# Starting the second pass of a fused decode-block forward and backward one iteration earlier

## The chip, the cores and the metric

The kernel runs on one core of one Trainium2 chip, as one launch. The metric is device time in microseconds (us), the median of several executions. Two sizes set most of it: tiles of 1 MiB of bfloat16 that are moved between HBM and the on-chip memory, and vector instructions of about 1 us each that work on them.

## What is computed

A transformer block for one decode token per batch row, and its whole gradient. Cut to what matters:

```python
B, D, H, Sk, Dh, Dff = 2, 640, 32, 4096, 128, 1728
def fwd(x, K, V, wq, wo, w1, w2):
    q = layernorm(x) @ wq                        # (B, H, Dh)
    p = softmax(einsum("bhd,bhkd->bhk", q, K) * Dh ** -0.5)
    o = einsum("bhk,bhkd->bhd", p, V)
    h = x + o.reshape(B, H * Dh) @ wo
    return h + relu(layernorm(h) @ w1) @ w2
out, vjp = jax.vjp(fwd, x, K, V, wq, wo, w1, w2)
return out, *vjp(grad_out)    # gradients of x, K, V, wq, wo, w1, w2
```

The caches K and V have 64 (batch, head) pairs of 1 MiB each; their gradients have the same size. Each pair's gradient is an outer product spread over the sequence, so it is written whole.

## The kernel before

**Two passes over the 64 pairs.** The first pass (`p1_iter`, lines 468 to 608) takes one new pair per iteration `i`, software-pipelined over three iterations: pair `i` is transposed on PE and scored, pair `i-1` gets its softmax weights (`ep`, line 540) and its weighted keys `pk` (line 486, on DVE), and pair `i-2` is reduced on PE against V (`m_part`, line 476). Each iteration loads one K and one V tile. The second pass (`p2_iter`, lines 892 to 970) takes head `j`: it needs V once more (tile `W`), and stores the gradients `gV` and `gK`, 1 MiB each, built on DVE at line 868 from the row `rb` (ACT, line 911). The last six V tiles of each batch row stay on chip (`KEPT`), and the second pass takes these first, so its heads run 26 to 31, then 0 to 25.

**The middle.** Between the passes of a batch row `b` stands `middle_gen(b)` (lines 771 to 842): the attention output, a layer norm, the hidden layer, the ReLU mask, the gradient through `w1`, the backward layer norm `ln_bwd` (lines 285 to 315), and then, by groups of heads (`go_group`, lines 711 to 742), the gradient of each head's output. Head `j` of the second pass can't start before its group is done. For batch row 0 the middle begins after iteration 33.

**The order of the work is written out by the program, at build time.** Each engine runs its instructions in the order in which they are emitted. `p1_iter` yields eight times in an iteration (steps k = 0 to 7); after each step the main loop emits some of the second pass, pumps the load queue, and lets the background (`bg`, the middle among it) emit as much as a credit allows: 0.8 a step in iterations 34 to `P2_AT - 1`, 0.2 a step in first-pass iterations from `P2_AT` on. A generator pays 0.5 for a plain yield. `wait(n)` (lines 152 to 157) holds the background back for n steps; it emits nothing. The long vector products of the middle (`ttr`, line 697) also need a slot from `turn()`: between the middle's start and `P2_AT` an iteration gives five (two at k = 1, one each at k = 3, 4 and 6). `bg_until` at the start of a head emits at once whatever that head still needs.

**The steps that matter here.** After the mask (`ghfc`, line 811) and a pause, `spread_some` (lines 655 to 664) turns a piece of `ghfc` into a row: PE transposes (line 661) into a PSUM bank, one copy on ACT (line 663) into `fbc`. Five `ttr` follow on it; this is done three times, with widths 640, 640 and 448. Then `ln_bwd`: sums on DVE, a pause, a column sum on PE (`colsum`, line 226), the rest on DVE; then the row `hbc`, spread in the same way; then `go_group` for heads 26 and 27: two `ttr`, a pause, `pair_rows` (lines 351 and 356), a pause, `d_ps` (lines 727 and 731) and five small DVE instructions to `GQc` (line 739). `csum`, `pr_ps` and `d_ps` all lie in PSUM bank 7 (role "mid").

**The second pass's start.** `P2_AT = H + 2 + M0_ITERS` (line 1182) is the first-pass iteration with head j = 0. From there every second iteration carries a head ("mixed") and the others none ("plain"), until i = 64, from where every step of the plan carries one. So heads stand in iterations 41, 43, ... 63, 64, 65, and heads 14 to 64 follow without a first pass. `P2_AT` also moves the end of the help that ACT gives with `pk` (`PK_ACT`, line 480), the engine of two small copies (lines 501 and 580), a K tile that goes over to the second pass (line 582), a PSUM bank (line 1284), the doubling of pauses (line 1312) and the start of batch row 1's output sums (line 1308).

**Transfers.** Loads are issued on SP's queue in one list (`queue`, lines 1197 to 1226), as soon as one of 13 homes of 1 MiB is free; during the mixed stage the stores are issued on POOL's queue. While six kept V tiles are held, seven homes are left for K and V. A K home comes free after the second `pk` instruction (line 582), a V home after line 604.

Of the kernel before, what the change touches and what calls it, by code (L numbers as in the profile page):

```python
# [15 lines left out]
def kernel(  # L16
# [41 lines left out]
    def f_kc(c):  # L58
        return 128 if c < NFF else F_rem
# [92 lines left out]
    def wait(n):  # L152

        end = step[0] + n * spread[0]
        while step[0] < end and not forced[0]:
            yield 0.0
        yield
# [34 lines left out]
    x2c = cols.tile([128, ND, B], BF16)  # L192
    rstd2 = cols.tile([128, B], FP32)
    gc = cols.tile([128, ND, B], BF16)
    h1c = cols.tile([128, ND, B], BF16)
    gh1c = cols.tile([128, ND, B], BF16)
# [26 lines left out]
    def colsum(src, n):  # L223

        t = pst([128, 16], FP32, "mid", "csum")
        nc.tensor.matmul(t[:, 0:n], lhsT=ones_f32, rhs=src, start=True, stop=True)
        return t

    def bc(ap, n):
        return ap[:, :, None].to_broadcast([128, ap.shape[1], n])  # L230
# [51 lines left out]
        nc.vector.tensor_tensor(out=xh.rearrange("p c b -> p b c"), in0=y_bf[:], in1=bc(rstd, ND), op=ALU.mult)  # L282
        yield from wait(3)

    def ln_bwd(gh, xh, rstd, add, dst, nb):

        lb = small if nb == 1 else fin
        def t3(name):
            return lb.tile([128, nb, ND], FP32, tag=f"lb_{name}{nb}", bufs=1, name=f"lb_{name}")
        xh_v = xh.rearrange("p c b -> p b c")  # L290
        prod = t3("prod")
        nc.vector.tensor_tensor(out=prod[:], in0=gh, in1=xh_v, op=ALU.mult)
        mm = lb.tile([128, 2, nb], FP32, tag=f"lb_mm{nb}", bufs=1, name="lb_mm")
        nc.vector.reduce_sum(out=mm[:, 0, :], in_=gh, axis=AX.X)
        nc.vector.reduce_sum(out=mm[:, 1, :], in_=prod[:], axis=AX.X)
        yield from wait(2)
        t = colsum(mm[:].rearrange("p a b -> p (a b)"), 2 * nb)
        yield
        nm = lb.tile([128, 2, nb], FP32, tag=f"lb_nm{nb}", bufs=1, name="lb_nm")
        nc.vector.tensor_scalar(out=nm[:].rearrange("p a b -> p (a b)"), in0=t[:, 0:2 * nb],  # L300
                                scalar1=-1.0 / D, scalar2=None, op0=ALU.mult)
        u1 = t3("u1")
        if nb == 1:
            nc.vector.scalar_tensor_tensor(out=u1[:, 0, :], in0=xh_v[:, 0, :], scalar=nm[:, 1, 0:1], in1=gh[:, 0, :],
                                           op0=ALU.mult, op1=ALU.add)
            nc.vector.tensor_scalar(out=u1[:, 0, :], in0=u1[:, 0, :], scalar1=nm[:, 0, 0:1], scalar2=rstd,
                                    op0=ALU.add, op1=ALU.mult)
        else:
            nc.vector.tensor_tensor(out=u1[:], in0=xh_v, in1=bc(nm[:, 1, :], ND), op=ALU.mult)
            nc.vector.tensor_tensor(out=u1[:], in0=u1[:], in1=gh, op=ALU.add)  # L310
            nc.vector.tensor_tensor(out=u1[:], in0=u1[:], in1=bc(nm[:, 0, :], ND), op=ALU.add)
            nc.vector.tensor_tensor(out=u1[:], in0=u1[:], in1=bc(rstd, ND), op=ALU.mult)
        nc.vector.tensor_tensor(out=dst.rearrange("p c b -> p b c"), in0=u1[:],
                                in1=add.rearrange("p c b -> p b c"), op=ALU.add)
        yield from wait(3)
# [298 lines left out]
    def o_group():  # L614
        b, g = divmod(o_next[0], H // OG)
        hs = slice(g * OG, g * OG + OG)
        nc.vector.tensor_tensor(out=OU[:, b, hs], in0=OU[:, b, hs], in1=rt[:, b, hs], op=ALU.mult)
        nc.vector.tensor_copy(out=OFc[:, hs, b], in_=OU[:, b, hs])
        o_next[0] += 1

    def a_group():

        b, g = divmod(a_next[0], H // OG)
        a_ps = pst([128, ND], FP32, "mid", "a_ps")
        for c in range(ND):
            for h in range(g * OG, g * OG + OG):
                nc.tensor.matmul(a_ps[:, c:c + 1], lhsT=wo_t[:, h, c * 128:(c + 1) * 128], rhs=OFc[:, h, b:b + 1],
                                 start=(h == g * OG), stop=(h == g * OG + OG - 1))
        nc.vector.tensor_tensor(out=asum[:, b, :], in0=asum[:, b, :], in1=a_ps[:], op=ALU.add)
        a_next[0] += 1  # L630
# [17 lines left out]
    def wide_row(name):  # L648
        return cols.tile([128, B * D], BF16, tag="wide_row", name=name)
# [121 lines left out]
    def middle_gen(b):  # L771
        if o_next[0] < (b + 1) * H // OG:
            o_group()
        u4[0] = wide_row("u")[:, 0:256].bitcast(FP32)
        nc.vector.tensor_reduce(out=u4[0], in_=u_bank[0][:].rearrange("p (s d) -> p d s", s=4),
                                axis=AX.X, op=ALU.add)
        yield
        if b:
            yield from wait(2)
        while a_next[0] < (b + 1) * H // OG:  # L780
            if a_next[0] == o_next[0]:
                o_group()
                yield
                yield
            a_group()
            yield
        at_bf = small.tile([128, ND], BF16, tag="at_bf", bufs=1, name="at_bf")
        nc.vector.tensor_copy(out=at_bf[:], in_=asum[:, b, :])
        nc.vector.tensor_tensor(out=h1c[:, :, b], in0=xg32[:, b, :], in1=at_bf[:], op=ALU.add)
        h32 = small.tile([128, 1, ND], FP32, tag="h32", bufs=1, name="h32")  # L790
        nc.vector.tensor_copy(out=h32[:, 0, :], in_=h1c[:, :, b])
        yield ("a", b)
        u_out(b)
        yield from ln_fwd(h32[:], 1, x2c[:, :, b:b + 1], rstd2[:, b:b + 1])
        wide = 32
        hf_w = pst([128, NF, wide], FP32, "mid", "hf_ps")
        hf_ps = hf_w[:, :, 0]
        for cf in range(NF):
            kc = f_kc(cf)
            for c in range(ND):  # L800
                nc.tensor.matmul(hf_w[0:kc, cf, :], lhsT=w1_t[:, c, cf * 128:cf * 128 + kc],
                                 rhs=x2c[:, c, b:b + 1].to_broadcast([128, wide]),
                                 start=(c == 0), stop=(c == ND - 1))
            yield 0.25
        nc.vector.tensor_scalar(out=acol[:, 0:NFF, b], in0=hf_ps[:, 0:NFF], scalar1=0.0, scalar2=None, op0=ALU.max)
        if F_rem:
            nc.vector.tensor_scalar(out=acol[0:F_rem, NFF, b:b + 1], in0=hf_ps[0:F_rem, NFF:NF],
                                    scalar1=0.0, scalar2=None, op0=ALU.max)
        mask = small.tile([128, NF], FP32, tag="mask", bufs=1, name="mask")
        nc.vector.tensor_single_scalar(out=mask[:], in_=acol[:, :, b], scalar=0.0, op=ALU.is_gt)  # L810
        nc.vector.tensor_tensor(out=ghfc[:, :, b], in0=ga[:, b, :], in1=mask[:], op=ALU.mult)
        yield from wait(3)
        fbc = wide_row("fbc")
        gx2 = small.tile([128, 1, ND], FP32, tag="gx2", bufs=1, name="gx2")
        gx2p = small.tile([128, ND, 3], FP32, tag="gx2p", bufs=1, name="gx2p")
        first_f = 0
        for k, n in enumerate((ND, ND, NF - 2 * ND)):
            row = fbc[:, (k % 2) * D:(k % 2 + 1) * D]
            w = spread_some(one(ghfc, b), k * ND, n, f_kc, row)
            yield  # L820
            for c in range(ND):
                yield from turn()
                part = w1_t[:, c, first_f:first_f + w]
                ttr(part, row[:, 0:w], gx2p[:, c, k:k + 1], w, part if b else later_heads())
                yield 0.85
            first_f += w
        nc.vector.reduce_sum(out=gx2[:, 0, :], in_=gx2p[:], axis=AX.X)
        yield ("w1", b)
        yield from ln_bwd(gx2[:], x2c[:, :, b:b + 1], rstd2[:, b:b + 1], gc[:, :, b:b + 1], gh1c[:, :, b:b + 1], 1)
        row = wide_row("hbc")  # L830
        hbc, junk = row[:, 0:D], row[:, D:2 * D]
        spread_some(one(gh1c, b), 0, ND, lambda c: 128, hbc)
        yield
        yield ("gh1", b)

        first = H - KEPT[b]
        bounds = [(first, first + 2), (first + 2, H)] if b == 0 else [(first, H)]
        bounds += [(h, min(first, h + GH)) for h in range(0, first, GH)]
        for h0, h1 in bounds:
            yield from go_group(b, h0, h1, hbc, junk)  # L840
        if b > 0:
            yield from mlp_out()
# [335 lines left out]
        forced[0] = False  # L1178

    EARLY = 2  # L1180
    M0_ITERS = 7
    P2_AT = H + 2 + M0_ITERS
    RATES = (0.2, 0.8, 0.2, 0.8, 0.45)
    RATE2 = 0.65
# [180 lines left out]
```

## Time and profile before

| what | value |
|---|---|
| median of 3 runs | 884.89 us (884.12 to 885.16) |
| the profiled execution | 885.37 us, span 883.6 us |
| busy share of the span: PE, DVE, ACT, POOL | 83%, 77%, 56%, 19% |
| moved by DMA | 361.86 MB, mean 410 GB/s |
| iterations 34 to 40 (middle of batch row 0) | some 44 us, about 207 to 251 us of the span |
| iteration 41 (mixed, head 0), iteration 42 (plain) | 9.0 us, 5.5 us, by line 604 on ACT |

The page cuts the span in 40 slices of 22.1 us and gives, for each, the busy share of each engine and the rate of the DMA. The windows view gives the same for stretches of one's choice; the timeline gives instructions with start, duration and, in brackets, how long the engine stood idle before them and what it then waited for. Line 604 on ACT runs once per first-pass iteration near its end, and serves as its clock. PE's busy share holds waits that are not shown as idle, so it says little here.

### The profile page before, as it was taken

The page shows a single profiled execution, that of the slowest core. Times are in us where ns is not written, and L with a number is a line of the kernel's source. Part 1 is how long each engine was busy: PE and PEld are TensorE (multiplying, and loading weights), DVE is VectorE, ACT ScalarE, POOL GpSimd, SP SyncE. Part 2 cuts the span into 40 slices and gives each one's busy share as a digit, 9 for nine tenths or more (in the row PEclk, how much of TensorE's full clock was granted, in tenths as well). Part 3 has the DMA queues.
Part 4 walks back from the last instruction along what each step waited for, and adds up shares of the span by engine and source line. Part 5 has one row for each costly group of instructions (what it writes and reads, how often), then busy time and mean ns, then how long its engine had stood idle before and what let it go on. Part 6 is the DMA issues. An engine that isn't in the chain of part 4 may idle for free.

```text
span 883.6 us, 24847 instructions
## 1 busy us (share of the span) xinstructions
PE 730.4 (83%) x10143; PEld 609.9 (69%) x10143; DVE 680.6 (77%) x1281; ACT 498.7 (56%) x1292; POOL 171.2 (19%) x291
## 2 busy tenths in 40 slices
PE   4999989999998998878868667777878888968780
PEld 4888878888887887767757556566757766654550
DVE  2666878866887897886787898778878679979861
ACT  1444434445776665545555868776656865656570
POOL 1344433443311010000022111111001111111110
PEclk9999999999999999999995657555555855565555
DMA  9999999999979999999999999999999999999995
GB/s 379 424 420 421 417 417 413 422 417 422 372 300 406 415 424 425 423 424 425 415 402 424 422 425 426 425 424 426 422 404 395 424 421 415 424 424 425 424 425 224
DMA packets 56035, 361.86 MB, mean 410 GB/s; under 512 B 5681, under 2 KB 11505, under 8 KB 15217
## 3 DMA queue, kind: packets, MB, share of 16 engines
q1 hardware_dynamic: 46968, 303.29, 82.7%
q0 software_dynamic: 8912, 56.97, 15.6%
q8 instruction: 80, 1.31, 0.5%
q14 instruction: 35, 0.28, 0.1%
q10 hardware_dynamic: 40, 0.01, 0.0%
HBM read 211.11 MB, written 149.13 MB: 408 GB/s over the span
## 4 chain that ended last, share of the span: by engine, by line
DMA 37%; PE 31%; DVE 18%; ACT 7%; issue 5%; ACTq 0%; SPq 0%; DVEq 0%; POOL 0%; POOLq 0%
DMA Vt<-in_A_v_cache_dram 18%; PE t_ps L440 13%; DMA out_dram<-gV 11%; PE m_ps L476 7%; DVE gV L868 4%; DVE gK L868 4%; DMA out_dram<-gK 4%; DMA Wt<-in_A_v_cache_dram 3%; ACT gV L958 3%; PE s_ps L453 2%; DVE pk L486 2%; PE u_ps L514 2%; DVE gxj L697 2%; ACT t_sb L445 2%; PE dp_ps L453 2%
## 5 line engine op out<-in xcount | busy, mean ns | idle before, releaser
L445 ACT COPY t_sb<-t_ps 128x512 f32<-128x512 f32 x479 | 273.1, 588 | 180.8 <-PE t_ps L440 176.6
L453 PEld LDWEIGHTS <-t_sb 128*128 128x128 bf16 x4096 | 178.2, 102 | 62.9 <-ACT t_sb L445 33.5
L440 PE MATMUL t_ps<-ident_f,Wt 128*128 128x128 f32 x832 | 196.0, 386 | 1.2 <-ACT t_sb L445 1.2
L476 PE MATMUL m_ps<-pk,Vt 128*128 128x129 bf16 x2048 | 170.4, 221 | 22.9 <-DMA Vt<-in_A_v_cache_dram 22.1
L486 DVE TENSOR_TENSOR pk<-Kt,ep 128x2048 bf16<-128x2048 bf16 (+1 forms) x128 | 152.8, 1194 | 45.7 <-ACT ep L540 30.5
L868 DVE TENSOR_TENSOR gK<-rb,gsp 128x2048 bf16<-128x2048 bf16 x128 | 153.1, 1224 | 19.8 <-DMA out_dram<-gV 17.8
L476 PEld LDWEIGHTS <-Vt 128*128 128x128 bf16 x2048 | 124.1, 98 | 54.0 <-issue 28.1
L440 PEld LDWEIGHTS t_ps<-ident_f,Wt 128*128 128x128 f32 x832 | 136.4, 200 | 28.9 <-issue 19.9
L868 DVE TENSOR_TENSOR gV<-rb,pp 128x2048 bf16<-128x2048 bf16 (+1 forms) x128 | 143.1, 1142 | 17.1 <-DMA out_dram<-gV 7.4
L440 PE MATMUL t_ps<-ident_f,Kt 128*128 128x128 f32 x1024 | 151.9, 281 | 2.4 <-DMA Kt<-in_A_k_cache_dram 1.7
L453 PE MATMUL dp_ps<-gom,t_sb 128*128 128x2 bf16 x2048 | 95.6, 168 | 22.6 <-ACT t_sb L445 22.1
L440 PEld LDWEIGHTS t_ps<-ident_f,Kt 128*128 128x128 f32 x1024 | 110.8, 142 | 5.0 <-ACT t_sb L445 2.7
L502 POOL COPY pk<-ep 128x16 bf16<-128x16 bf16 x80 | 83.6, 1046 | 155.1 <-ACT ep L540 73.9
L453 PE MATMUL s_ps<-qm,t_sb 128*128 128x2 bf16 x2048 | 87.0, 163 | 1.5 <-DVE t_sb L443 1.5
L1012 ACT CAST ot<-o_ps 128x512 bf16<-128x512 f32 (+3 forms) x152 | 67.7, 492 | 7.6 <-PE o_ps L1006 6.8
L604 ACT CAST MT<-m_ps 128x128 bf16<-128x128 f32 x64 | 17.0, 266 | 93.8 <-PE m_ps L476 93.7
L913 POOL COPY pp<-P_bf 128x64 bf16<-128x64 bf16 x64 | 34.7, 544 | 141.5 <-DVE gV L868 122.4
L911 ACT ACTIVATE rb<-dp_ps,rt 128x256 bf16<-128x256 f32 x64 | 30.3, 473 | 50.4 <-PE dp_ps L906 50.2
L697 DVE CUSTOM_DVE_ANT_0 hbc<-wo_t,hbc 128x640 bf16<-128x640 bf16 x64 | 53.0, 828 | 0.8 <-ACT hbc L663 0.6
L958 ACT ACTIVATE gV<-rb,pa 128x128 bf16<-128x128 bf16 x152 | 46.5, 391 | 5.7 <-POOL pa L917 3.1
L697 DVE CUSTOM_DVE_ANT_0 gxj<-wqs,gqr 128x1024 bf16<-128x1024 bf16 x40 | 49.0, 1225 | 0.2
L440 PE MATMUL t_ps<-ident_f,Vt 128*128 128x128 f32 x192 | 40.5, 352 | 1.5 <-ACT t_sb L445 1.5
(208 smaller groups left out, 709.4 us busy)
## 6 DMA issues: line engine op xcount, KB each, us to landing
Kt<-in_A_k_cache_dram SPq DMA_DIRECT2D x64, 1024.0 KB, 19.6
Vt<-in_A_v_cache_dram SPq DMA_DIRECT2D x64, 1024.0 KB, 15.6
Wt<-in_A_v_cache_dram SPq DMA_DIRECT2D x52, 1024.0 KB, 16.7
out_dram<-gK SPq DMA_DIRECT2D x48, 1024.0 KB, 17.3
out_dram<-gV SPq DMA_DIRECT2D x47, 1024.0 KB, 17.9
out_dram<-gV POOLq DMA_DIRECT2D x17, 1024.0 KB, 9.8
out_dram<-gK POOLq DMA_DIRECT2D x16, 1024.0 KB, 10.5
wq_t<-in_A_wq_dram SPq DMA_DIRECT2D x5, 1024.0 KB, 7.9
```

The costliest lines, as they stand in the source:

```text
L440: nc.tensor.transpose(t_ps[:, j, :], natf[:, 2 * cc:2 * cc + 2, :].rearrange("p c k -> p (c k)"), ident_f[:])
L445: nc.scalar.copy(out=t_sb[:], in_=t_ps[:])
L453: nc.tensor.matmul(dst[:, sc:sc + 2], lhsT=v[:, j, :, par], rhs=vecs[:, par, :], start=(par == 0), stop=(par == 1))
L476: nc.tensor.matmul(r["m"][:, 0:129], lhsT=r["V"][:, sc, :], rhs=r["pk"][sc // HALF][:, sc % HALF, 0:129], start=(sc == 0), stop=(sc == NSC ...
L486: nc.vector.tensor_tensor(out=p["pk"][k][:, 0:n, 0:128].rearrange("p s (a two) -> p s a two", two=2), in0=p["K"][:, sl, :].rearrange("p s ...
L502: nc.gpsimd.tensor_copy(out=col, in_=e)
L697: nc.vector.tensor_tensor_reduce(out=junk[0:kc, 0:width], in0=in0, in1=in1, scale=1.0, scalar=0.0, op0=ALU.mult, op1=ALU.add, accum_out=acc)
L868: nc.vector.tensor_tensor(out=pairs_view(dst[:, sl, :]), in0=row.rearrange("p (a two) -> p a two", two=2)[:, None, :, :].to_broadcast([128 ...
L911: nc.scalar.activation(out=rb[:], in_=bank[:, 128:384], func=ACT.Copy, scale=rt[:, b, h:h + 1])
L913: nc.gpsimd.tensor_copy(out=pp[:], in_=P_bf[:, b * H + h, :, None].to_broadcast([128, NSC, 2]))
L958: nc.scalar.activation(out=gV[:, NSC - act + k, :], in_=c["rb"][:, 0:128], func=ACT.Copy, scale=pa[:, k:k + 1])
L1012: nc.scalar.copy(out=ot[0:P, k, n0:n0 + nn], in_=o_ps[0:P, 0:nn])
```

## The change

Four constants. The pause between the mask and the first spread is one step for batch row 0, not three. `ln_bwd` gets an argument `less`, which takes one step off its first pause for batch row 0 (`1 - b` is 1 there; the final layer norm's call keeps 0). `M0_ITERS` is 6, not 7, so `P2_AT` is 40, not 41: heads 0 to 11 stand in iterations 40, 42, ... 62, iteration 63 carries none, and heads 12 and 13 stay in 64 and 65. No instruction is added or removed by it, apart from those that depend on `P2_AT`.

```diff
-    def ln_bwd(gh, xh, rstd, add, dst, nb):
+    def ln_bwd(gh, xh, rstd, add, dst, nb, less=0):
...
-        yield from wait(2)
+        yield from wait(2 - less)
         t = colsum(mm[:].rearrange("p a b -> p (a b)"), 2 * nb)
...
         nc.vector.tensor_tensor(out=ghfc[:, :, b], in0=ga[:, b, :], in1=mask[:], op=ALU.mult)
-        yield from wait(3)
+        yield from wait(3 if b else 1)
         fbc = wide_row("fbc")
...
-        yield from ln_bwd(gx2[:], x2c[:, :, b:b + 1], rstd2[:, b:b + 1], gc[:, :, b:b + 1], gh1c[:, :, b:b + 1], 1)
+        yield from ln_bwd(gx2[:], x2c[:, :, b:b + 1], rstd2[:, b:b + 1], gc[:, :, b:b + 1], gh1c[:, :, b:b + 1], 1, 1 - b)
...
-    M0_ITERS = 7
+    M0_ITERS = 6
```

## The prediction

> **What bounds the kernel now.** I read the page's slices first, then the windows around their dips, then the timelines of DVE, PE and SP there.
>
> The DMA and GB/s rows of the page:
>
> ```profile
> DMA  9999999999979999999999999999999999999995
> GB/s 379 424 420 421 417 417 413 422 417 422 372 300 406 415 424 425 423 424 425 415 402 424 422 425 426 425 424 426 422 404 395 424 421 415 424 424 425 424 425 224
> ```
>
> The transfers run at 424 GB/s nearly all the time; engines wait for them. The end therefore moves by what the DMA loses below that rate, wherever it loses it. The large dip is in slices 11 and 12 (221 to 265 us); small ones follow in 20 and 21. The windows (columns: stretch, sum, then busy time and instructions of PE, PEld, DVE, ACT, POOL, then clock, DMA share, GB/s):
>
> ```profile
> 220.00:230.00 10.00, 9.18 (x162) 8.26 (x160) 6.59 (x20) 7.01 (x20) 2.87 (x4) 1.00 0.90 364
> 230.00:240.00 10.00, 9.69 (x164) 8.11 (x161) 9.89 (x23) 8.52 (x29) 3.45 (x8) 1.00 0.99 386
> 240.00:250.00 10.00, 9.71 (x163) 8.14 (x161) 8.81 (x32) 8.42 (x24) 2.24 (x7) 1.00 0.94 360
> 250.00:260.00 10.00, 9.64 (x162) 8.68 (x160) 8.92 (x21) 6.36 (x19) 1.12 (x4) 1.00 0.59 237
> ...
> 430.00:440.00 10.00, 8.16 (x144) 7.07 (x143) 7.01 (x20) 4.99 (x12) 0.78 (x2) 1.00 0.99 410
> 440.00:450.00 10.00, 8.20 (x137) 7.26 (x135) 9.86 (x18) 5.05 (x16) 2.02 (x3) 1.00 0.99 397
> 450.00:460.00 10.00, 7.17 (x115) 5.83 (x114) 5.82 (x8) 5.14 (x11) 1.31 (x4) 1.00 1.01 393
> ```
>
> From 230 to 250 us DVE is the fullest engine (9.89 and 8.81 of 10) while the DMA is short of work: the middle of batch row 0 makes the first pass slower than its loads. SP's timeline shows the hole after that:
>
> ```profile
> 246.59 0.61 SPq L461 DMA_DIRECT2D Vt<-in_A_v_cache_dram  x1
> 251.37 0.33 SPq L461 DMA_DIRECT2D Kt<-in_A_k_cache_dram  x1
> 259.54 0.33 SPq L461 DMA_DIRECT2D Vt<-in_A_v_cache_dram  x1
> ```
>
> Eight microseconds without a load, in the first mixed iteration; the first store is issued at 258.60 on POOL. DVE's timeline gives the beat of iterations 36, 37 and 41 (`nb`, line 533, starts each one's loop) and the idle that the middle leaves:
>
> ```profile
> 222.07 0.29 DVE L533 TENSOR_REDUCE nb<-s_ps 128x1 f32<-128x128 f32 x1 [0.43 <-PE s_ps L531]
> ...
> 225.24 0.83 DVE L697 CUSTOM_DVE_ANT_0 P_bf<-w_t,fbc 128x640 bf16<-128x640 bf16 x1 [1.31 <-ACT fbc L663]
> ...
> 228.91 0.29 DVE L533 TENSOR_REDUCE nb<-s_ps 128x1 f32<-128x128 f32 x1
> ...
> 253.19 0.29 DVE L533 TENSOR_REDUCE nb<-s_ps 128x1 f32<-128x128 f32 x1
> ```
>
> PE's, the start of iterations 40 and 41 and the moment from which I measure the second pass:
>
> ```profile
> 245.33 1.04 PE L440 MATMUL t_ps<-ident_f,Kt 128*128 128x128 f32 x8
> ...
> 251.38 1.07 PE L440 MATMUL t_ps<-ident_f,Kt 128*128 128x128 f32 x8
> 252.60 0.23 PE L531 MATMUL s_ps<-neg_ident,rmax 128*128 128x128 bf16 x1
> ```
>
> **Does the middle fit?** I counted credits, pauses and slots through the steps of both versions. Before: first spread at iteration 36 step 2, the fifteen `ttr` from (36,3) to (39,1), `colsum` (39,4), `ttr` of heads 26 and 27 (40,1), `pair_rows` (40,3), `d_ps` (40,5): the order that the timeline has. After: spread at (36,0), so that the two slots at k = 1 of iteration 36 are used; `ttr` from (36,1) to (38,6); `colsum` (38,7) thanks to the shorter pause; `hbc` at (39,2); heads 26 and 27 at (39,3) and (39,4); `pair_rows` (39,6). Only `d_ps` and its five DVE instructions are left, forced out at the start of iteration 40. So it fits, by a hair.
>
> **What moves and what it costs.**
>
> *The pauses* emit nothing and cost nothing themselves; what they covered was latency between engines, priced below.
>
> *The shortened middle: how much earlier does head 0 start?* I lay DVE's and PE's queues out anew with the durations of before. Iteration 36: the spread's five transposes (0.28 us) now stand ahead of line 531, so `nb` starts at 222.4, not 222.07. The copies of the two K groups occupy ACT from 221.63 to 222.70; `fbc` (0.70) follows, to 223.4. Two `ttr` (0.82 each) to 225.1, first `pk` 0.74, two `ttr`, second `pk` 1.14, `rmax` 0.1, a fifth `ttr`: `nb` of 37 at 229.5 instead of 228.91, with five products done instead of three. Iteration 37 has what 37 had (6.16 us from 228.91 to 235.07), so `nb` of 38 at 235.7. Iteration 38 has five narrow products: before it had two wide and three narrow in 5.55 us (235.07 to 240.62), a wide one is 0.2 longer, so 5.15, and the sums ahead of `colsum` add 0.5 (242.14 to 242.65): 241.35. Now the **new wait**: `colsum` stands ahead of iteration 39's K transposes on PE. It takes 0.33 after the sums, the transposes 0.95, then lines 531 and 533: `nb` of 39 at 243.1. DVE meanwhile waits some 0.6 for the sum (0.54 before at line 300). Iteration 39: in 36 it took 3.2 us from `nb` to the first product after a spread, 0.8 of it a late V tile (PE's idle at 222.85), so 2.3 here: head 26 at 245.4. Two products 1.7, two small instructions 0.3, `pk` 1.14, `rmax` 0.1, `gom` casts 0.5: 249.05. **Second new wait**: `d_ps` uses the bank that the casts read, so PE stands until 249.05, runs `d_ps` (0.35) and only then the transposes of iteration 40 (0.95). Line 531 of iteration 40 at 250.4, against 252.60 in iteration 41 before. Head 0 starts **2.2 us earlier**. Bounds: 1.0 if both waits hit harder by the 0.6 that such a wait was here; 6.05 if a whole iteration went (245.33 to 251.38). I take 2.2, as each term has its row.
>
> *The first-pass iteration that is no longer in the middle.* Iteration 40's load of K and V, 2 x 1024 KB = 2.10 MB, was done before head 0 and now has to be done beside the second pass, where the rate is 424 GB/s already: **4.95 us**. It appears as the plain iteration 63. The DVE work of a plain iteration (2.3 us) lies under these transfers.
>
> *What else P2_AT moves*: heads 0 to 11 go one iteration forward with their 24 stores on POOL and, for heads 6 to 11, six W loads on SP, which pass one K and one V in the list. Order changes, bytes don't; the hole of the first mixed iteration moves with it (same homes, same first stores), worth 4.4 us before and after. Iteration 40 loses ACT's six `pk` pieces (1.86 us on ACT) and DVE's `pk` grows from 0.74 to 1.14; POOL's two column copies go to ACT (0.27 each). That is 0.4 us of DVE in a stage that waits for transfers: nothing; without that cover 0.4.
>
> *The end of the first pass*: heads stood in 63, 64 and 65 in a row, DVE at 9.86 of 10, and the DMA lost (14 + 27 + 31) / 424 x 10 = 1.7 us from 430 to 460. With iteration 63 plain, DVE has 2.3 us of work there instead of 7. Bounds: 0 (from 64 on nothing changes) to 1.7 back. I take 0.5, half of what 430 to 450 lost, as the loss after 450 stands where heads 12 and 13 wait for their own stores.
>
> **Sum**: 4.95 - 2.2 - 0.5 = +2.25 us on 885.37, so 887.6; that execution lies 0.5 above the median, so against the median **887.1 us**, +0.25%. With the middle's bounds near their rows (1.2 to 3.2, end 0 to 1): 885.6 to 888.6.
>
> **Rivals.**
>
> *A whole iteration goes (faster).* The middle's idle on DVE takes up the two products at no cost, head 0 starts 6.05 us earlier, and the row of three heads gives its 1.7 us back: 4.95 - 6.05 - 1.7 = -2.8, 882.1 us. It wins from the point where these two together pass 6.7 us. For it: DVE idles 2.5 us in iteration 36 and 0.54 and 0.32 later. Against it: 36 gains only what lies between two waits, and two new PE waits stand where the pauses were. [...] 20%.
>
> *Waits cancel (no change).* The casts come early enough that `d_ps` holds nothing up: head 0 starts 3.5 us earlier, the end gives 0.7: +0.75, 885.6 us. For it: both waits are priced from single rows of 0.5 to 0.6 us, and the casts may come earlier than my queue has them. 18%.
>
> *The waits cost more (slower).* Each spread now stands at steps where PE and ACT are fuller; head 0 gains only 1.0 and the end nothing: +3.95, 888.8 us. 13%.
>
> *It doesn't fit*: two products are forced out too, 1.64 us more ahead of head 0: 4.95 - 0.5 = +4.45, 889.3 us. The count speaks against it. 4%.
>
> **Numbers.** My forecast has 45%. A measurement of this kernel can tell about 0.2% (1.8 us) from no change, so the borders are 883.1 and 886.7. Of the forecast's own 45, 8 lie under 886.7. Slower: 37 + 13 + 4 = 54%; within: 8 + 18 = 26%; faster: 20%. The range 882.6 to 889.2 takes in part of the first rival (11 left out below) and all but some 5 above.
>
> **What would show it.** Line 531 of iteration 40 near 250.4, with PE idle before `csum` and `d_ps`; first spread's `ttr` right after `nb` of 36; five `ttr` in 36 to 38; GB/s from 220 to 250 lower than before (the same per-iteration bytes in longer iterations); the hole of some 8 us between loads again, ahead of the first store; 430 to 460 a little fuller. If line 531 of iteration 40 comes before 247.6 the first sum is wrong; if the stretch after 290 us isn't full of transfers, the 4.95 is.

## The result, and the profile after

The changed kernel takes 888.08 us (median of 10 runs, 886.52 to 891.95) against 885.04 us for the kernel before (10 runs, 884.10 to 886.74): a ratio of 1.0035, 95% interval 1.0023 to 1.0047, so 3 us slower. The profiled execution has a span of 886.3 us against 883.6.

The page's DMA and GB/s rows of the changed kernel:

```profile
DMA  9999999999969999999999999999999999999995
GB/s 378 426 419 421 417 417 412 423 416 422 361 234 380 424 423 424 424 425 425 424 406 422 423 425 426 425 420 425 422 410 402 423 425 421 421 417 424 424 424 251
```

The dip in slices 11 and 12 is deeper (361 and 234, where it was 372 and 300), the one in slices 20 and 21 is shallower (424 and 406, where it was 415 and 402), and the last slice carries more (251 against 224). The same stretches in the windows view, with the columns of before:

```profile
220.00:230.00 10.00, 9.32 (x161) 8.24 (x157) 7.40 (x22) 7.18 (x21) 1.58 (x4) 1.00 0.91 365
230.00:240.00 10.00, 9.36 (x163) 7.67 (x161) 9.86 (x24) 8.30 (x27) 2.37 (x8) 1.00 0.93 366
240.00:250.00 10.00, 7.48 (x98) 6.67 (x98) 6.61 (x21) 5.35 (x17) 1.94 (x5) 0.83 0.75 290
250.00:260.00 10.00, 9.18 (x127) 8.67 (x128) 7.33 (x21) 4.95 (x12) 0.70 (x1) 0.83 0.38 133
...
430.00:440.00 10.00, 9.44 (x159) 8.34 (x157) 9.22 (x23) 5.47 (x16) 0.77 (x2) 1.00 1.01 424
440.00:450.00 10.00, 9.25 (x160) 7.56 (x159) 8.38 (x18) 5.86 (x19) 1.31 (x3) 1.00 1.01 415
450.00:460.00 10.00, 6.67 (x99) 5.80 (x92) 7.28 (x10) 3.51 (x9) 0.77 (x2) 0.86 1.00 393
```

From 240 to 260 us the transfers fell from 360 and 237 GB/s to 290 and 133, and DVE is no longer full there: 8.81 and 8.92 of 10 became 6.61 and 7.33. ACT falls too, and PE, at 7.48 and 9.18, shows a granted clock of 0.83. The account against 424 GB/s: from 220 to 290 us the mean is 363 GB/s before and 330 after, so (424 - 330) x 70 / 424 = 15.5 us are lost instead of 10.1, 5.4 more. From 430 to 470 it is 406 and 414, 0.8 less lost; from 860 to the end 236 over 23.6 us and 279 over 26.3 us, 1.5 less. That leaves +3.1, against 2.7 in the spans. The stretches between, 290 to 430 and 470 to 860, have the same mean rate in both profiles to within 1 GB/s.

PE's timeline of the changed kernel, iterations 39 and 40:

```profile
241.78 0.38 PE L226 MATMUL csum<-lb_mm,ones_f32c 128*128 128x2 f32 x2 [2.08 <-DVE lb_mm L295]
242.03 1.75 PE L440 MATMUL t_ps<-ident_f,Kt 128*128 128x128 f32 x8
...
250.82 0.35 PE L727 MATMUL d_ps<-pr,ones_f32c 128*128 128x2 f32 x2 [1.55 <-DVE gom L356]
251.03 0.19 PE L731 MATMUL d_ps<-goc,MT 128*128 128x1 bf16 x2
251.08 1.07 PE L440 MATMUL t_ps<-ident_f,Kt 128*128 128x128 f32 x8
251.99 0.22 PE L531 MATMUL s_ps<-neg_ident,rmax 128*128 128x128 bf16 x1
```

Both forecast waits stand there, 2.08 us ahead of `csum` and 1.55 us ahead of `d_ps`, and behind the first the K transposes take 1.75 us instead of 1.07. Line 531 of the iteration with head 0 comes at 251.99 where it came at 252.60: one first-pass iteration fewer, and the second pass starts 0.6 us earlier (0.9 if iteration 36 is laid at the same time in both, as in the table further down). The chain that ended last shows why. From the backward layer norm on it goes through every step of the middle, and between these steps through first-pass work that is emitted ahead of the next one (the K transposes, lines 531, 476 and 445, and `pk`):

```profile
241.60 0.14 DVE lb_mm L295
241.78 0.38 PE csum L226 x2
242.17 1.62 PE t_ps L440 x8
...
243.89 0.87 PE m_ps L476 x8
244.75 0.87 PE t_ps L440 x4
...
246.28 0.60 ACT hbc L663
246.91 0.82 DVE hbc L697
247.78 0.83 DVE hbc L697
...
248.95 1.23 DVE pk L486
...
250.82 0.35 PE d_ps L727 x2
```

Of the 9.6 us from 241.60 to 251.17 some 5.4 are such first-pass work.

The loads, on SP's timeline:

```profile
240.97 0.38 SPq L461 DMA_DIRECT2D Vt<-in_A_v_cache_dram  x1
249.07 0.33 SPq L461 DMA_DIRECT2D Kt<-in_A_k_cache_dram  x1
259.80 0.33 SPq L461 DMA_DIRECT2D Vt<-in_A_v_cache_dram  x1
```

Two gaps of 8.1 and 10.7 us with one load between them, where before there were 4.8 and 8.2. A home comes free only as first-pass iterations advance, and iterations 38 and 39 take 8.3 and 9.1 us each (line 440 to line 440), against 6.2 and 6.1 in the kernel before:

```profile
233.08 1.07 PE L440 MATMUL t_ps<-ident_f,Kt 128*128 128x128 f32 x8
239.26 1.07 PE L440 MATMUL t_ps<-ident_f,Kt 128*128 128x128 f32 x8
```

### The profile page after: what moved, and what is told of

Same layout as the page of the kernel before. It is cut to its first block, busy times and chain, and to the rows that moved or that the text cites. A ratio compares the mean times of both kernels' runs of the same rounds, so it can differ in the third digit from the quotient of the medians.

```text
span 886.3 us, 24829 instructions
## 1 busy us (share of the span) xinstructions
PE 741.3 (84%) x10143; PEld 620.4 (70%) x10143; DVE 681.7 (77%) x1282; ACT 497.0 (56%) x1288; POOL 165.9 (19%) x287
## 4 chain that ended last, share of the span: by engine, by line
PE 38%; DMA 32%; DVE 16%; ACT 7%; issue 4%; ACTq 0%; DVEq 0%; SPq 0%
PE t_ps L440 17%; DMA Vt<-in_A_v_cache_dram 14%; DMA out_dram<-gV 12%; PE m_ps L476 9%; DMA out_dram<-gK 5%; DVE gK L868 4%; DVE gV L868 4%; PE s_ps L453 3%; ACT gV L958 3%; DVE pk L486 3%; ACT t_sb L445 2%; PE u_ps L514 2%; PE dp_ps L453 2%; PE o_ps L1006 2%; DVE hbc L697 1%
## 5 line engine op out<-in xcount | busy, mean ns | idle before, releaser
L453 PEld LDWEIGHTS <-t_sb 128*128 128x128 bf16 x4096 | 180.6, 103 | 63.7 <-ACT t_sb L445 34.0
L440 PE MATMUL t_ps<-ident_f,Kt 128*128 128x128 f32 x1024 | 158.7, 289 | 2.9 <-DMA Kt<-in_A_k_cache_dram 2.3
L440 PEld LDWEIGHTS t_ps<-ident_f,Kt 128*128 128x128 f32 x1024 | 115.3, 146 | 6.6 <-ACT t_sb L445 3.7
L913 POOL COPY pp<-P_bf 128x64 bf16<-128x64 bf16 x64 | 32.6, 513 | 136.8 <-DVE gV L868 116.2
L911 ACT ACTIVATE rb<-dp_ps,rt 128x256 bf16<-128x256 f32 x64 | 30.2, 472 | 39.8 <-PE dp_ps L906 39.6
L882 DVE SCALAR_TENSOR_TENSOR gsp<-dp_ps,negdot,P_bf 128x64 bf16<-128x64 f32 x64 | 17.9, 280 | 37.1 <-PE dp_ps L453 36.9
```

The lines of the kernel that those rows point to most:

```text
L440: nc.tensor.transpose(t_ps[:, j, :], natf[:, 2 * cc:2 * cc + 2, :].rearrange("p c k -> p (c k)"), ident_f[:])
L453: nc.tensor.matmul(dst[:, sc:sc + 2], lhsT=v[:, j, :, par], rhs=vecs[:, par, :], start=(par == 0), stop=(par == 1))
L911: nc.scalar.activation(out=rb[:], in_=bank[:, 128:384], func=ACT.Copy, scale=rt[:, b, h:h + 1])
L913: nc.gpsimd.tensor_copy(out=pp[:], in_=P_bf[:, b * H + h, :, None].to_broadcast([128, NSC, 2]))
```

## The experiments

Each was compared with the kernel before on the same chip; its median there was 884.5 to 884.9 us. Two theories were set against each other. "Loads": a six-iteration middle moves 4.95 us of loads into the stage that is full of transfers, and gets back only what head 0 starts earlier. "Waits": the two new PE waits and the slower PE clock behind them (0.52 to 0.62 where it was 1.00) are the cost, and without them six iterations win. The kernels stand in the order in which they argue; a table follows.

**The pauses alone**, with seven iterations:

```diff
-    M0_ITERS = 6
+    M0_ITERS = 7
```

> Both pauses shortened, seven iterations of the middle as before. Theory 'loads' (a six-iteration middle costs 4.95 us of loads that move into the full stage, less what head 0 starts earlier, less 0.5 to 0.75 at the end of the first pass): head 0 starts where it did (line 531 of iteration 41 at 252 to 253 us) and the time is that of before, 884 to 886 us. Rival 'waits' (the cost of the change is the two new waits on PE and its lower clock after the first): the wait ahead of csum is there here too, so about half of the 3 us is paid, 886 to 887 us.

Measured: 889.81 us, ratio 1.0061 (1.0044 to 1.0077). Both expectations missed: by the medians this part of the change costs more than the whole (4.9 us against 3.0; the intervals just touch). PE's timeline:

```profile
249.48 0.22 PE L531 MATMUL s_ps<-neg_ident,rmax 128*128 128x128 bf16 x1
...
256.94 0.36 PE L727 MATMUL d_ps<-pr,ones_f32c 128*128 128x4 f32 x2 [0.83 <-DVE gom L356]
257.26 0.22 PE L531 MATMUL s_ps<-neg_ident,rmax 128*128 128x128 bf16 x1
```

The middle is done with heads 26 and 27 by iteration 40, and its credit and slots then go to the next group: all four products of heads 28 to 31 and their `d_ps` are emitted ahead of head 0. Iteration 40 takes 7.8 us, and head 0 starts at 257.26, 4.7 us later than before, with the same loads done. A delay of that size, without loads that move, fits the loss.

**The same with heads 28 to 31 held back** until the second pass has begun:

```diff
         for h0, h1 in bounds:
+            while b == 0 and h0 == first + 2 and spread[0] == 1 and not forced[0]:
+                yield 0.0
             yield from go_group(b, h0, h1, hbc, junk)
```

> Both pauses shortened, seven iterations, heads 28 to 31 held back until the second pass. The pauses alone lost 4.9 us; their trace shows these heads' products and their d_ps ahead of head 0 (line 531 of iteration 40 at 249.5, of iteration 41 at 257.3, 7.8 us). 'Loads': iteration 40 becomes a plain one of 5 to 5.5 us, line 531 of iteration 41 at about 254.7, some 2 us later than before: 886.5 to 887.5. Rival 'the pauses themselves cost' (csum's wait and the PE clock): still 889 to 890.

Measured: 889.32 us, 1.0050 (1.0037 to 1.0063): in the rival's range of 889 to 890, and "loads" missed. Line 531 of iteration 41 came at 256.16, 1.1 us earlier than without the hold but 3.6 later than before. Iteration 40 did become plain (5.4 us from 250.76 to 256.16), but iterations 38 and 39 are long here too: 8.25 us, as without the hold, and 7.0 us, where it was 5.5 without the hold. PE's granted clock was 0.81, 0.50 and 0.83 from 242 to 248 here, and 1.00 in the profile without the hold. So with seven iterations the shortened pauses cost even without these heads. That the cost comes from where they put `csum` and `d_ps` on PE is argued, not shown, and how much of what the hold saved was lost again to the clock isn't separated.

**The iteration alone**, with the pauses of before:

```diff
-    M0_ITERS = 7
+    M0_ITERS = 6
```

> Six iterations of the middle with the pauses of before, so that both products of heads 26 and 27, pair_rows and d_ps are forced out at the start of iteration 40, ahead of its K transposes. 'Loads': head 0 starts later than in the change (line 531 of iteration 40 at 252.5 to 254, line 531 of iteration 41 later than 262), so slower than the change: 888.5 to 890. Rival 'pauses' (in the change the shortened pauses are what costs, as they alone cost 4.9 us with seven iterations): 885 to 887, faster than the change.

Measured: 888.14 us, 1.0043 (1.0031 to 1.0056): the changed kernel's time, above the range of "pauses" and 0.4 us below that of "loads". Though the products of heads 26 and 27, `pair_rows` and `d_ps` are all forced out ahead of iteration 40, line 531 stands at 251.45, earlier than "loads" had it. So at six iterations the two pauses neither help nor hurt by as much as could be told; "pauses" falls. PE waits here too, 2.72 us ahead of `pr_ps`.

**The wait ahead of `csum` undone**, by giving the backward layer norm its pause back:

```diff
-gh1c[:, :, b:b + 1], 1, 1 - b)
+gh1c[:, :, b:b + 1], 1, 0)
```

> The change without the shorter pause of the backward layer norm, so that csum comes behind the K transposes of iteration 39 on PE instead of ahead of them. Both theories: the 2.08 us of PE idle ahead of csum go, and the PE clock stays at 1.00 from 240 to 250. 'Loads': line 531 of iteration 40 comes 1 to 1.5 us earlier (250.5 to 251), and the time falls by as much, to 886.5 to 887. 'Waits': half of the penalty goes, 886.5; the two part only in the next run but one.

Measured: 888.05 us, 1.0034 (1.0021 to 1.0048), no gain, and both expectations missed. The clock stayed at 1.00 and line 531 of iteration 40 came at 250.57, as expected, and yet the time didn't follow. The idle didn't go either: PE now waited 1.14 us ahead of `csum` and 1.89 ahead of `pr_ps`. The profiled execution was the fastest of the seven timed ones (886.19 us, against 888.05 in the middle), so its timeline, and its full clock, may not be typical.

**The wait ahead of `d_ps` moved** behind iteration 40's first transposes:

```diff
             if j < NP1:
+            if j < NP1 and (i is None or j > 0):
                 bg_until(("go", *turns[j]))
...
         for k, _ in enumerate(p1_iter(i, i < H + 1, 0)):
+            if k == 0 and j == 0:
+                bg_until(("go", *turns[j]))
```

(the first line with "if" is replaced by the second)

> The change, with the rest of head 26's gradient (d_ps and its five DVE instructions) emitted behind the first K transposes of iteration 40, not ahead of them. 'Loads': PE no longer stands 1.55 us ahead of the transposes, line 531 of iteration 40 at about 250.7, time 886.8 to 887.3. 'Waits': the other half of the penalty goes, 886.5.

Measured: 886.60 us, 1.0022 (1.0012 to 1.0033). The time is the value that "waits" gave (886.5) and lies 0.2 us below the range of "loads". The wait shrank from 1.55 to 0.63 us and the time by some 1.2 us by the two ratios, but their intervals overlap, so the gain isn't certain.

**Both together:**

> The change with both repairs. 'Loads': head 0 starts some 2.5 to 3.3 us earlier than before the change, still less than the 4.95 us of loads, so 886 to 887 us: no version of a six-iteration middle with this much DVE work in it beats before. 'Waits': with both waits gone the freed DVE idle shows, and it is faster than before, 883 to 884.

Measured: 887.04 us, 1.0026 (1.0013 to 1.0038): at the upper end of the "loads" range, and clearly not faster than before. As it was put, "waits" falls. But the waits weren't gone; PE's timeline shows what happens to a wait that is taken away:

```profile
240.34 1.07 PE L440 MATMUL t_ps<-ident_f,Kt 128*128 128x128 f32 x8
242.54 0.38 PE L226 MATMUL csum<-lb_mm,ones_f32c 128*128 128x2 f32 x2 [1.14 <-DVE lb_mm L295]
...
249.40 0.21 PE L351 MATMUL pr_ps<-goc,sel 128*128 128x2 bf16 x2 [1.89 <-DVE goc L720]
249.47 1.95 PE L440 MATMUL t_ps<-ident_f,Kt 128*128 128x128 f32 x8
```

Iteration 38 is short again (5.8 us, from 234.54 to 240.34), but iteration 39 now takes 9.1 us (240.34 to 249.47): the transposes went ahead, and PE stood at the next instructions that needed the middle, 1.14 us ahead of `csum` and 1.89 ahead of `pr_ps`. The clock fell here as well, to 0.96 from 240 to 250 us and 0.87 from 250 to 260. No run shows six iterations with the full sum and without such waits.

**One iteration more**, with heads 28 to 31 held back, so that iteration 41 is plain:

```diff
-    M0_ITERS = 7
+    M0_ITERS = 8
```

> Eight iterations of the middle, the pauses of before, heads 28 to 31 held back, so that iteration 41 is a plain one with no work of the middle in it. 'Loads': head 0 starts 5.0 to 5.5 us less 0.8 later, and 4.95 us of loads are done by then: 884 to 885.5, no change. Rival 'each iteration by which the second pass starts later costs its whole length': 889 to 890.

Measured: 885.50 us, 1.0009 (0.9999 to 1.0019): no change that can be told, as "loads" has it (its range ends at 885.5), and far from the rival's 889 to 890. PE's timeline, iterations 41 and 42:

```profile
251.30 1.07 PE L440 MATMUL t_ps<-ident_f,Kt 128*128 128x128 f32 x8
...
256.85 1.07 PE L440 MATMUL t_ps<-ident_f,Kt 128*128 128x128 f32 x8
```

A first-pass iteration with nothing of the middle in it takes 5.55 us by line 440 (5.26 by line 531), 0.6 or 0.3 more than its 4.95 us of loads. So an iteration added to the middle is worth some 0.3 to 0.6 us if the rest stays as it is, not 6.05. That the same holds for one taken away is inferred from it.

**Heads 28 to 31 held back in the kernel before**, the control for it:

> Before, with the products of heads 28 to 31 held back until the second pass has begun (one product of 0.82 us leaves iteration 40). 'Loads': head 0 starts up to 0.8 us earlier and no load moves, so 884.0 to 885.0. Rival 'order of DVE work doesn't matter, the sum does': 885 as before.

Measured: 885.01 us, 1.0006 (0.9996 to 1.0016), no change; line 531 of iteration 41 at 252.50, as before. The two expectations lie too close together for this to choose between them. The product taken away stood behind `rmax`, off the path.

**Less DVE work in the middle**, with seven and with six iterations: only the first 64 columns of each piece are multiplied and summed, and the rest of the sum is left out (15 products of 0.22 us in place of ten of 0.82 and five of 0.62).

```diff
-                ttr(part, row[:, 0:w], gx2p[:, c, k:k + 1], w, part if b else later_heads())
+                tw = w if b else 64
+                ttr(part[:, 0:tw], row[:, 0:tw], gx2p[:, c, k:k + 1], tw, part if b else later_heads())
```

> Before, with the products of batch row 0's masked gradient with w1 taken over the first 64 columns of each piece only (the rest of that sum is left out), which takes some 8 us of DVE work out of iterations 36 to 39. 'Loads': these iterations fall from 6 us towards the 5 to 5.5 us that loads and PE need, head 0 starts 3 to 4 us earlier with the same loads done: 881 to 882.5. Rival 'DVE isn't what makes the middle slow': 884 to 885.

> The change, with the same part of that sum left out. Now the iteration that is dropped is 5 to 5.5 us long and has little of the middle's DVE work, so that what it held doesn't stretch the other six. 'Loads': head 0 starts 4 to 5 us earlier than with seven narrow, which is about the 4.95 us of loads that move: from 1 us faster to 1 us slower than seven narrow. Rival 'six iterations cost by themselves (their two PE waits, the order of the stores)': 2 to 3 us slower than seven narrow, as with the full sum.

Measured: seven 884.07 us, 0.9983 (0.9968 to 0.9998); six 884.86 us, 0.9997 (0.9983 to 1.0012). With the DVE work gone six and seven differ by 0.8 us by the medians (1.2 by the ratios), at the edge of the "loads" range and well under the 3 us of the full sum; head 0 came 3.5 us earlier with six than with seven (line 531 at 248.45 against 251.96), not 4 to 5. But seven gained only 0.6 us by the medians (1.5 by the ratio, with 2.8 at the interval's end), less than "loads" had: "DVE isn't what makes the middle slow" comes out right for seven iterations. DVE's timeline, from the mask to the end of heads 26 and 27, for seven narrow, six narrow, the kernel before and the changed kernel:

```profile
222.01 0.18 DVE L811 TENSOR_TENSOR ghfc<-ga,mask 128x14 bf16<-128x14 f32 x1
...
251.64 0.17 DVE L739 TENSOR_SCALAR GQc<-ud 128x2 bf16<-128x2 f32 x1
```

```profile
221.76 0.18 DVE L811 TENSOR_TENSOR ghfc<-ga,mask 128x14 bf16<-128x14 f32 x1
...
248.38 0.17 DVE L739 TENSOR_SCALAR GQc<-ud 128x2 bf16<-128x2 f32 x1
```

```profile
221.46 0.18 DVE L811 TENSOR_TENSOR ghfc<-ga,mask 128x14 bf16<-128x14 f32 x1
...
252.28 0.17 DVE L739 TENSOR_SCALAR GQc<-ud 128x2 bf16<-128x2 f32 x1
```

```profile
221.74 0.18 DVE L811 TENSOR_TENSOR ghfc<-ga,mask 128x14 bf16<-128x14 f32 x1
...
251.91 0.17 DVE L739 TENSOR_SCALAR GQc<-ud 128x2 bf16<-128x2 f32 x1
```

From start to start that is 29.6 us and 26.6 us, and with the full sum 30.8 us before and 30.2 us in the changed kernel. With seven iterations eight microseconds less on DVE shortened the stretch by 1.2 us; the middle is then paced by the steps of the first pass, in which its pauses, credits and slots are counted, so DVE has room. With six, taking the work out saved some 3.5 us there. Not all of that need be DVE's: PE's clock stayed at 1.00 in six narrow, while it fell to 0.56 in the changed kernel. With the `csum` pause back, whose profile has the full sum and a clock of 1.00, the stretch is 28.9 us (221.62 to 250.49), so some 1.3 of the 3.5 us may be the clock and where `csum` stands.

**A different relief for DVE**: ACT takes eight pieces of `pk`, not six, with seven iterations.

```diff
-    PK_ACT = 6
+    PK_ACT = 8
```

> Before, with ACT taking eight of the 32 pieces of pk in the middle, not six (lines 480 and 491): 0.14 us less on DVE in each of iterations 34 to 40, 0.62 us more on ACT, which had 8.4 of 10 from 230 to 250. 'Loads': head 0 starts up to 0.7 us earlier, 884 to 885. Rival 'ACT becomes the bound': its iteration is 5.2 + 0.6 = 5.8 us of work plus waits, 885 to 887.

Measured: 885.11 us, 1.0004 (0.9987 to 1.0021): no change by the interval. Line 531 of iteration 41 came at 253.22, 0.6 later and not earlier, but the profiled execution was this kernel's slowest (888.56 us).

All in one table. "Account" is 4.95 us for each first-pass iteration fewer in the middle, plus the shift of line 531 in the iteration after head 0's (261.04 before), each timeline set so that iteration 36 starts where it did before (line 440 at 220.88). It comes from one profiled execution each, and some of these lie 2 us and more from their kernel's median (both, 888.95 against 887.04; eight on ACT, 888.56 against 885.11).

```profile
220.88 1.09 PE L440 MATMUL t_ps<-ident_f,Kt 128*128 128x128 f32 x8
...
261.04 0.22 PE L531 MATMUL s_ps<-neg_ident,rmax 128*128 128x128 bf16 x1
```

| kernel | iterations | account, us | measured (ratio - 1) x 885, us |
|---|---|---|---|
| the change | 6 | 5.3 | +3.1 |
| six alone | 6 | 5.2 | +3.8 |
| `csum` pause back | 6 | 3.0 | +3.0 |
| head 0 forced late | 6 | 3.4 | +1.9 |
| both | 6 | 3.6 | +2.3 |
| pauses alone | 7 | 4.4 | +5.4 |
| pauses, heads held | 7 | 3.0 | +4.4 |
| eight, heads held | 8 | 0.3 | +0.8 |
| before, heads held | 7 | 0.0 | +0.5 |
| seven narrow | 7 | -1.2 | -1.5 |
| six narrow | 6 | 0.7 | -0.3 |
| eight `pk` pieces on ACT | 7 | 0.7 | +0.4 |

The account has the sign of every row whose interval leaves out "no change", and a size to within some 2 us. All six-iteration rows but one come out lower than it, and of the six others four come out higher, by 0.5 to 1.4, and two lower by 0.3. That fits the end of the first pass in part: from 430 to 470 us the five six-iteration kernels with the full sum moved 414, 415, 416, 406 and 410 GB/s and six narrow 419, before 406, and the pauses alone, the pauses with heads held, and eight 394, 407 and 392. That part is read from single profiles and wasn't isolated by a run.

"Loads" was not a good forecast of each time: it missed by 0.2 us or more in six of the eleven runs, and with seven iterations and shortened pauses it missed by far. What speaks for it are the three runs in which the rivals lay far apart: both pauses moved, eight iterations, and six against seven narrow. No variant that computes the whole sum beat the kernel before, so none is offered in its place.

## Why the prediction was right, and where it wasn't

**Direction and size.** Forecast +2.25 us, 887.1; measured +3.0, 888.08, inside the likeliest case's own range of 885.6 to 888.6. The mechanism was the one forecast: 4.95 us of loads move into the stage that is full of transfers, and head 0's earlier start doesn't pay for them. Three terms were off. Head 0 gained 0.9 us (0.6 as the profiles stand), not 2.2; its own iteration took 1.2 us longer, where nothing was put down; and the end of the first pass and the end of the span together gave back 2.3 us, not 0.5. That makes 4.95 - 0.9 + 1.2 - 2.3 = 2.95, from one profile of each kernel. The first two terms add 2.5 us to the forecast and the third takes away 1.8, so that the total came so close is in part luck.

**Does it fit.** Right, step by step. DVE's timeline of the changed kernel has `nb` of iterations 36 and 37 and the first product where the new layout put them; the last line, `nb` of iteration 40, comes late:

```profile
222.62 0.29 DVE L533 TENSOR_REDUCE nb<-s_ps 128x1 f32<-128x128 f32 x1 [0.70 <-PE s_ps L531]
223.60 0.82 DVE L697 CUSTOM_DVE_ANT_0 P_bf<-w_t,fbc 128x640 bf16<-128x640 bf16 x1 [0.69 <-ACT fbc L663]
...
229.64 0.28 DVE L533 TENSOR_REDUCE nb<-s_ps 128x1 f32<-128x128 f32 x1
...
252.25 0.29 DVE L533 TENSOR_REDUCE nb<-s_ps 128x1 f32<-128x128 f32 x1 [0.16 <-PE s_ps L531]
```

Forecast 229.5 for `nb` of 37, measured 229.64; forecast 235.7 for 38, measured 235.83.

**How much earlier head 0 starts.** The term that was mis-sized most: forecast 2.2 us with a lower bound of 1.0, measured 0.6 (0.9 when aligned), below the bound. After iteration 38 each step ran late: `nb` of 39 at 243.93 (forecast 243.1), head 26's product at 246.91 (245.4), the casts' end at 250.67 (249.05), line 531 at 251.99 (250.4). The forecast had both waits but priced what follows the first by rows with a clock of 1.00: the eight K transposes behind it, at a clock of 0.56 from 242 to 244 us, took 1.75 us where I had 0.95, and from `nb` to head 26's product it was 3.0 us where I had 2.3. Of the 1.6 us by which line 531 came late, 0.4 were there before the first wait (the sums ended at 241.73, forecast 241.35) and 1.1 were added from there to head 26's product.

**4.95 us of loads.** Right: a plain iteration added to the middle left the time where it was.

**The hole of the first mixed iteration**, "worth 4.4 us before and after": wrong. From 250 to 260 us the DMA lost 6.9 us against 424 GB/s instead of 4.4, and the gap between loads grew from 8.2 to 10.7 us. Of these 2.6 us, 1.7 lie ahead of head 0: its iteration's line 531 comes 2.9 us after the K load where it came 1.2 after it. The other 0.9 lie behind: iteration 40 took 9.7 us (251.99 to 261.65 at line 531) where 41 took 8.4. Behind the second wait PE's clock fell again, and it was 1.00 there before:

```profile
252.00:254.00 2.00, 2.00 (x19) 2.00 (x17) 0.82 (x3) 1.47 (x4) 0.00 (x0) 0.62 0.55 229
254.00:256.00 2.00, 2.00 (x28) 1.94 (x27) 2.00 (x4) 1.47 (x5) 0.00 (x0) 0.52 0.00 0
```

In the three six-iteration profiles with a clock of 1.00 in head 0's iteration (`csum` pause back, head 0 forced late, six narrow) that iteration took 8.6 us, and 9.9 with six alone, whose clock was 0.50 to 0.66 from 250 to 256. So most of the 1.2 us goes with the clock.

**The end of the first pass**: forecast 0.5 us back, measured 0.8 from 430 to 470, and another 1.5 us at the end of the span that I hadn't named and that no run here explains.

**DVE as the fullest engine, and the middle as DVE-bound**: only half right. In the prediction's own rows PE is fuller from 240 to 250 us (9.71 against 8.81); it was set aside because its busy share holds waits (at a clock of 1.00 the eight K transposes from 251.38 on are shown as 1.07 us, and those from 259.86 on, among which PEld waits 0.29 us for ACT's `t_sb`, as 1.34). But the chain that ended last in the kernel before runs on PE from 222.85 to 244.00 us, but for 1.4 us around 233 to 234. For seven iterations eight microseconds less on DVE brought 0.6 us by the medians; much of its fullness was work that fitted beside PE's iterations of 5.5 to 6.1 us (line 440 to line 440 in seven narrow). At six the chain from the mask to head 0 decides, with the first-pass work that stands in it.

**The rivals.** "A whole iteration goes" fell: 36 did take five products at little cost, but the middle didn't shrink with the iterations beside it (30.2 us against 30.8). Head 0 came 0.6 us earlier (0.9 when aligned), not 6.05; an iteration beside the middle was worth some 0.3 to 0.6 us, by the run with eight. "Waits cancel" fell with the two waits of 2.08 and 1.55 us. "The waits cost more" (888.8) came as near as the forecast, 0.7 us off where the forecast was 1.0 off, and its gain of 1.0 us for head 0 was the better one; that the end would give nothing was wrong. "It doesn't fit" fell with the count; its sum, moreover, leaves out the 0.56 us that its own terms leave to head 0 (2.2 less 1.64), with which it is 888.8 too.

## What to carry to other kernels

Ask of a stage not how long its iterations are but what sets its length. Here the stretch from the mask to head 26's gradient took 28.6 to 31.5 us in every kernel with the full sum, with six, seven or eight iterations in the middle; an iteration beside it was nearly free (some 0.3 to 0.6 us with eight), and taking one out moved its loads to a place where they are paid in full (an estimated 4.95 us at 424 GB/s). And here a wait that was moved came back at the next instruction that needed a result of the middle: with both moved PE stood 1.14 us ahead of `csum` and 1.89 ahead of `pr_ps`.

## What the runs showed of the hardware

Behind a PE wait of about 2.1 us ahead of `csum` the granted clock was lower in some profiled executions and not in others. The windows from 242 to 246 us of the changed kernel, then of the pauses alone, whose wait was 2.07 us:

```profile
242.00:244.00 2.00, 2.00 (x14) 1.94 (x14) 0.92 (x5) 0.71 (x2) 0.00 (x0) 0.56 0.87 336
244.00:246.00 2.00, 2.00 (x26) 1.94 (x25) 1.04 (x2) 1.06 (x4) 0.98 (x2) 0.58 0.98 385
```

```profile
242.00:244.00 2.00, 2.00 (x28) 1.98 (x29) 1.14 (x5) 1.30 (x4) 0.00 (x0) 1.00 0.89 352
244.00:246.00 2.00, 2.00 (x40) 1.40 (x36) 1.51 (x2) 1.77 (x5) 0.98 (x2) 1.00 1.03 430
```

The clock column reads 0.56 and 0.58 against 1.00, and PE got 14 and 26 matmuls done in 2 us instead of 28 and 40. With head 0 forced late (2.08 us) the clock fell too, to 0.67 and 0.50, and with the pauses and the heads held (2.07 us) to 0.81 and 0.50. Shorter waits show the same: behind 1.55 us ahead of `d_ps` the changed kernel's clock was 0.62 and 0.52, behind 1.56 us in six narrow it stayed at 1.00. So the same length of wait came with a lower clock in some profiled executions and with the full one in others. No run here varied such a wait alone, so what decides between the two isn't shown.
